# A recurrence feeding two gated MLPs on one core: the scratch word of the weight conversion moves to a PSUM bank, and two copies change their route

## The chip, the cores and the metric

One core of a Trainium2 chip runs the whole program. The metric is the device time of one execution in microseconds (us), lower is better. In the profile the engines are PE (TensorE), DVE (VectorE), ACT (ScalarE), POOL (GpSimd) and SP (SyncE, which here only issues DMAs; ACT issues DMAs too, and a letter q behind an engine's name stands for its sequencer).

## The reference

Batch 4, 8 heads, 768 time steps, head dimension 40. A linear recurrence gives one 320-wide row for each of 3072 tokens, and two MLPs follow on these rows.

```python
for t in range(S):
    y[:, :, t] = einsum('bhd,bhde->bhe', r_t, state)
    Sa = einsum('bhde,bhe->bhd', state, a_t)
    state = state * w_t - einsum('bhd,bhe->bhde', Sa, b_t) + einsum('bhd,bhe->bhde', v_t, k_t)
x = y.transpose(0, 2, 1, 3).reshape(3072, 320)
x = gate(x @ w_in) @ w_out                      # d_ff 2048; gate: 0, (h+1)^2/4 or h
out = (silu(x @ w_gate) * (x @ w_val)) @ w_out2  # d_ff 1536
```

The weights arrive as 8-byte numbers and are turned into float32 by bit operations, then into a high and a low float16 part.

## The kernel before

**Tiling.** Time is cut into 12 chunks of 64 steps. A chunk has four pieces of work, one for each batch entry, so there are 48 of them, numbered n = 4c + j. For each n, `p_tasks` prepares operands and the 64x64 products (tiles `ars`, `art`, `kbs`, `kbT`, `lkt`, `l21`), and `m_tasks` solves the triangular system of the chunk and carries the state on. For each chunk, `inv_tasks` inverts the 32x32 diagonal blocks of all 32 batch-head pairs in 62 short DVE instructions (lines 919 and 924), one pair behind the other. The two MLPs of a chunk (`in1`, `in2`, `outp`) follow when its rows are there: PE matmuls at lines 1181 and 1245, with ACT, DVE and POOL passes between them.

**Order.** All work is entered as tasks (engine, estimated cost, priority, buffers used) in a `Plan`. Its list scheduler runs when the program is built and fixes the order of every engine's instructions, from the costs written at each task and from pools of buffers; it repeats forward and backward passes and keeps the order with the earliest modelled end. A pool hands out a buffer in order of priority, and a task that finds none waits. DMAs go to SP's or ACT's queue, whichever the model finds free; on the chip each queue issues strictly in that order.

**The weights.** `wpiece` loads one of 58 pieces of raw words into a buffer of pool `wr` and works in three DVE instructions (`bits`, q = 0, 1, 2, lines 613, 617, 623): shift the upper word and mask it, put its top bits back, join the lower word's bits. By the code 20 pieces are 128x512, 28 are 128x320 and 10 are 128x256 (for those, line 623 runs twice on 64 partitions). The scratch word is the first part of the piece's buffer in pool `wu`, in SBUF, and the result of q = 2 goes to the same buffer. Then ACT (lines 643, 635) and POOL or DVE (lines 544, 546) split it into the two float16 parts.

**The solve.** Each `m_tasks` holds a PSUM bank of pool `px` (two banks; the first four solves may use the `ph` banks) from its first matmuls (line 1040) through two half solves: ACT line 1063, DVE and POOL copies of the half's right side, PE line 1050 with the inverse (`tt`), ACT line 1077 and DVE line 546 for the result, PE line 1056 between the halves. The inverse of a chunk goes from `ub` to DRAM (`tsd`, four copies, line 945) and back to `tt` (two copies for each pair of solves, lines 1011 and 1015). At its end a solve leaves the new state: `ss` by ACT and DVE, a transposed copy `s0t` (line 1154), and a stack `s0s` of three blocks of 40 partitions (high, low, high part) made from a POOL copy into `sr` (line 1158, high and low part) and three copies from SBUF to SBUF (line 1163). The solve n + 4 reads `s0s` at line 1133.

**Buffers around it.** `art`, `kbs`, `lkt` and `l21` have six buffers each, and two more (one for `lkt`) that serve n = 4 to 7 at the start and n >= 8 only once `pad` has run, which waits for the last weights. So until then the preparation of n needs the buffers of the solve n - 6.

Of the kernel before, what the change touches and what calls it, by code (L numbers as in the profile page):

```python
# [9 lines left out]
F16 = mybir.dt.float16  # L10
# [312 lines left out]
def tile_recurrence__then__gated_mlps(  # L323
# [64 lines left out]
    def pst(name, n):  # L388
        ts = [pp.tile([128, 512], F32, name=f"{name}{i}") for i in range(n)]
        K.pool(name, ts)  # L390
        return ts
# [28 lines left out]
    sbt("xs", [128, H, D], F16, 2)  # L420
    sbt("tt", [128, 2, 2, H, HC], F16, 1)
    gfs = sbt("gf", [128, H, C], F32, 1)
    K.pool("sr", [gfs[0][0:D].bitcast(F16).rearrange("p h t -> p (h t)")[:, 0:2 * HD].rearrange(
        "p (l h d) -> p l h d", l=2, h=H)])
    sbt("pf", [128, H, C], F32, 1)
    mx = sbt("mx", [128, 36 * NT], F16)
    K.pool("xt", [mx[:, 6 * NT * i:6 * NT * (i + 1)].rearrange("p (a t) -> p a t", a=6)
# [27 lines left out]
            "p (h x) -> p h x", h=H)], early)  # L455
    K.spare("gf", [mx[:, 7168:8192].bitcast(F32).rearrange("p (h t) -> p h t", h=H)], early)
    px = pst("px", 2)
    pst("pg", 2)
    ph = pst("ph", 2)
    po = [pp.tile([128, 512], F32, name=f"po{i}") for i in range(2)]  # L460
# [57 lines left out]
    def c_ps(n):  # L518
        return 0.14 + n * 0.9e-3

    def DMA(emit, dma, cost=0.78, **kw):
        T("DQ", cost, lambda q: emit(nc.scalar if q == "ACT" else nc.sync), dma=dma, **kw)
# [62 lines left out]
    def wpiece(names, key, src, n, m, dst_hi, dst_lo, scale, p, fit, r=()):  # L585
# [3 lines left out]
            "low": (0,), "high": (1,), "free": (2,), "late": (3, 4)}[f]]  # L589
        K.pools["wu"]["fit"][key] = [x for f in fit for x in {  # L590
            "low": (0, 4), "high": (1, 5), "free": (2,), "late": (3,)}[f] if m <= 320 or x < 4]
        raw, ux = [("wr", key)], [("wu", key)]
        shape = list(dst_hi.shape)

# [13 lines left out]
            e.dma_start(out=G("wr", key)[:, 0:2 * mw].bitcast(I32), in_=src)  # L608

        def bits(q):  # L610
            t = G("wu", key)[:, 0:mw].bitcast(I32)
            if q == 0:
                v_.tensor_scalar(  # L613
                    out=t, in0=x(1), scalar1=3, scalar2=0x3FFFFFFF,
                    op0=ALU.logical_shift_left, op1=ALU.bitwise_and)
            elif q == 1:
                v_.scalar_tensor_tensor(  # L617
                    out=t, in0=x(1), scalar=-(1 << 30), in1=t, op0=ALU.bitwise_and,
                    op1=ALU.bitwise_or)
            else:  # L620
                for i in range(2 if low else 1):
                    z = slice(64 * i, 64 * i + 64) if low else slice(0, 128)
                    v_.scalar_tensor_tensor(  # L623
                        out=u().bitcast(I32)[:, i * mw:i * mw + mw], in0=x(0)[z], scalar=29,
                        in1=t[z], op0=ALU.logical_shift_right, op1=ALU.bitwise_or)
# [10 lines left out]

        DMA(load, r=r, w=[(key, 0)], use=raw, p=p, dma=0.00365 * m * n / 128)
        for q in range(3):
            T("DVE", (0.08 + mw * 0.52e-3, 0.06 + mw * 1.04e-3, (0.21 if low else 0.06) + m * 1.04e-3)[q],
              lambda q=q: bits(q), r=[(key, q)],  # L640
              w=[(key, q + 1)], use=raw + ux, p=p)
        if pool:
            T("ACT", c_s(m), lambda: s_.activation(
                out=u(), in_=u(), func=AF.Copy, scale=scale0), r=[(key, 3)], w=[(key, 4)], use=ux, p=p)
# [243 lines left out]

    def inv_tasks(c, p):
        key = ("i", c)  # L890
        tsd[c] = dr.tile([2, 2, HC, BH, HC], F16, name=f"tsd{c}")
        ub, pm = [("ub", key)], [("pg", key)]

        def L():
# [8 lines left out]
        def T16():  # L903
            return G("ub", key)[:, 0:512].bitcast(F16).rearrange(
                "p (l m t) -> p l m t", l=2, t=HC)
# [34 lines left out]
        T("DVE", c_v(512), lambda: split(T16()[:, 1], M(), 2.0**8, T16()[:, 0]),  # L940
          r=[(key, "h")], w=[(key, "l")], use=ub + pm, p=p)

        def st(e, g, hf):
            l0 = 64 * g + 32 * hf
            e.dma_start(
                out=tsd[c].rearrange("f l (m g) b t -> f g b l m t", g=2)[hf, g],
                in_=T16()[l0:l0 + 32])

        for g in range(2):
            for hf in range(2):  # L950
                DMA(lambda e, g=g, hf=hf: st(e, g, hf), r=[(key, "l")], w=[("tsd", c)], use=ub,
                    p=p - 20, dma=0.73, cost=0.68)

    def x_tile(name, key):
        t = G(name, key)
# [24 lines left out]
    def m_tasks(n, p):  # L980
# [15 lines left out]
        if j % 2 == 0:  # L996
# [8 lines left out]
            if not last:  # L1005
# [4 lines left out]
            td = tsd[c][:, :, :, ps]  # L1010
            DMA(lambda e: e.dma_start(
                out=G("tt", mp)[0:64].rearrange("p f j h t -> p f (j h t)"),
                in_=td.rearrange("f l s b t -> (l s) f (b t)")),
                r=[("tsd", c)], w=[(mp, "tt")], use=TT, p=p - 3, dma=0.5)
            DMA(lambda e: e.dma_start(
                out=G("tt", mp)[64:96].rearrange("p f j h t -> p f (j h t)"),
                in_=td[:, 0].rearrange("f s b t -> s f (b t)")),
                r=[("tsd", c)], w=[(mp, "tt")], use=TT, p=p - 3, dma=0.25, cost=0.68)

        T("ACT", c_s(HD), lambda: s_.activation(  # L1020
# [116 lines left out]
        if not last:  # L1137
            y = lambda: hd(G(pg, (key, "y")))[q]
            if c:
# [15 lines left out]
                out=s0t[j], in_=flat(G("ss", key)[64:112])),  # L1155
                r=[("ss", n)], w=[("s0t", n)], use=SS, p=p, dma=0.57)
            SR = [("sr", key)]
            T("Pool", c_ps(2 * HD), lambda: p_.tensor_copy(
                out=G("sr", key),
                in_=G("ss", key)[q, :, 0:2 * D].rearrange("p h (l d) -> p l h d", l=2)),  # L1160
              r=[("ss", n)], w=[(key, "sr")], use=SS + SR, p=p + 8)
            for i in range(3):
                DMA(lambda e, i=i: e.dma_start(
                    out=s0s[j][D * i:D * i + D], in_=G("sr", key)[:, i % 2]),
                    r=[(key, "sr")], w=[("s0s", n)], use=SR, p=p + 8, dma=0.12, cost=0.45)
        xk = ("x", c, j // 2)
        xf = lambda: G("pf", (key, "x"))[vr].rearrange("p h t -> p (h t)")[:, 0:HD]
        XF = [("pf", (key, "x"))]
# [123 lines left out]
    for i in range(NP1):  # L1292
# [4 lines left out]
        for x in ps:  # L1297
            n = len(first)
            first.append(wpiece(
                *x, p=-WLEAD + WSTEP * n, fit=("low", "high", "free") if n < NW1 else ("low", "high")))  # L1300
    late, low, high = [], list(first), list(first)
    free = [("dec", c) for c in range(NCH)] + [("f", c) for c in range(NCH - 1)] + first[:NW1]
    for i, k in W2:
        if k < 2:
# [105 lines left out]
```

## Time and profile before

| | us |
|---|---|
| median of three runs | 1190.2 (1187.24 to 1194.36) |
| the profiled execution, its time | 1187.51 |
| the profiled execution, its span | 1185.5 |
| PE busy in the span | 914.2 (77%) |
| DVE busy | 808.5 (68%) |
| ACT busy | 738.7 (62%) |
| POOL busy | 707.6 (60%) |

The span is cut into stretches with different limits: the first 380 us, in which weights are converted; the middle, in which chunks follow one another at an even pace; and the end, in which only MLPs are left. Busy shares are to be read for each stretch alone. "The chain of work that ended last" follows the last instruction back through what released each step, so an engine's or line's share of it is the part of the span that it holds up.

### The profile page before, as it was taken

How to read it: one execution, taken by the hardware profiler on the slowest of the kernel's cores; microseconds unless marked ns; L12 is line 12 of the kernel's file. 1: busy time of each engine (PE TensorE's matmuls, PEld its weight loads, DVE VectorE, ACT ScalarE, POOL GpSimd, SP SyncE). 2: the span in 40 equal slices, each digit the busy share in tenths (PEclk: the TensorE clock that was granted, in tenths of full speed). 3: DMA queues.
4: the chain of work that ended last, by engine and by line, in shares of the span. 5: the costliest groups of instructions: out<-in, count | busy, mean ns of one | idle time of the engine just before them, and what ended most of it. 6: DMA issues, size and time to landing. Idle time of an engine off the chain costs nothing.

```text
span 1185.5 us, 29632 instructions
## 1 busy us (share of the span) xinstructions
PE 914.2 (77%) x11328; PEld 746.2 (63%) x11328; DVE 808.5 (68%) x1888; ACT 738.7 (62%) x1380; POOL 707.6 (60%) x952
## 2 busy tenths in 40 slices
PE   0321245645668698899998989999999899999998
PEld 0220233434457477677776777778778778788887
DVE  8779896998978677486684784867848668442111
ACT  0874575655676576775866857768668675553422
POOL 4698758544668567566675666676666644342321
PEclk9999999767989899999999999999999999999999
DMA  7954776738676757676567586774766743211000
GB/s 218 229 155 124 224 153 146 175 96 179 163 152 140 152 101 141 139 124 135 104 120 127 113 134 126 129 152 94 133 120 132 123 93 67 66 18 30 12 14 23
DMA packets 381522, 144.61 MB, mean 122 GB/s; under 512 B 345140, under 2 KB 358100, under 8 KB 381380
## 3 DMA queue, kind: packets, MB, share of 16 engines
q1 hardware_dynamic: 364416, 126.34, 51.3%
q10 hardware_dynamic: 16964, 16.39, 6.1%
q8 instruction: 88, 1.44, 0.5%
q14 instruction: 54, 0.44, 0.1%
HBM read 74.87 MB, written 18.14 MB: 78 GB/s over the span
## 4 chain that ended last, share of the span: by engine, by line
DVE 29%; PE 24%; DMA 15%; ACT 10%; POOL 9%; issue 7%; SPq 4%; ACTq 1%; POOLq 0%; DVEq 0%
PE ph L1181 12%; PE po L1245 9%; DVE pg L924 3%; DVE ub L919 3%; DMA ub<-lsd 3%; DVE vss L546 3%; DMA x2t<-mx 2%; DVE wo L623 2%; POOL ldp L550 2%; DVE wo L617 2%; DVE mx L1217 1%; DMA tsd<-ub 1%; POOL wv L550 1%; ACT ss L1146 1%; DVE wo L613 1%
## 5 line engine op out<-in xcount | busy, mean ns | idle before, releaser
L1245 PE MATMUL po<-wo,mx 128*128 128x320 f16 x2016 | 310.6, 302 | 15.8 <-POOL mx L544 8.4
L544 POOL TENSOR_TENSOR mx<-mx 128x512 f16<-128x512 f32 x168 | 196.6, 1172 | 188.8 <-ACT mx L1201 177.0
L1245 PEld LDWEIGHTS <-mx 128*128 128x128 f16 x2016 | 191.6, 98 | 88.2 <-POOL mx L544 11.2
L1181 PE MATMUL ph<-mx,w 128*128 128x256 f16 x1536 | 201.6, 285 | 54.7 <-DVE mx L1217 33.3
L1181 PEld LDWEIGHTS <-w 128*128 128x128 f16 x1536 | 150.7, 101 | 81.5 <-issue 53.5
L1201 ACT CAST mx<-mx 128x512 f16<-128x512 f32 x168 | 102.5, 615 | 81.3 <-DVE mx L1231 38.5
L1181 PE MATMUL ph<-x2t,wv 128*128 128x256 f16 x1152 | 140.2, 272 | 3.8 <-DVE mx L1231 3.1
L1181 PE MATMUL ph<-x2t,wg 128*128 128x256 f16 x1152 | 139.5, 272 | 2.7 <-DVE mx L1217 1.4
L1217 DVE SCALAR_TENSOR_TENSOR mx<-ph,mx 128x512 f32<-128x512 f32 x96 | 66.0, 688 | 91.2 <-ACT mx L1214 90.7
L1181 PEld LDWEIGHTS <-wv 128*128 128x128 f16 x1152 | 110.8, 98 | 17.9 <-issue 4.6
L1181 PEld LDWEIGHTS <-wg 128*128 128x128 f16 x1152 | 109.5, 98 | 17.1 <-issue 2.9
L919 DVE SCALAR_TENSOR_TENSOR ub<-ub,pg 128x126 f32<-128x126 f32 (+22 forms) x372 | 91.4, 246 | 15.3 <-DMA ub<-lsd 7.9
L924 DVE TENSOR_TENSOR pg<-pg,ub 128x126 f32<-128x126 f32 (+22 forms) x372 | 95.2, 256 | 7.1
L1231 DVE SCALAR_TENSOR_TENSOR mx<-ph,mx 128x512 f32<-128x512 f32 x72 | 49.3, 685 | 70.7 <-PE ph L1181 66.7
L550 POOL TENSOR_TENSOR ldp<-ldp 64x320 f32<-64x320 f32 (+1 forms) x90 | 79.8, 894 | 12.0 <-DMA ldp<-was 7.2
L1077 ACT ACTIVATE vss<-px 32x640 f16<-32x640 f32 x88 | 59.9, 693 | 28.0 <-PE px L1050 20.2
L1213 ACT ACTIVATE mx<-ph 128x512 f32<-128x512 f32 x96 | 57.1, 595 | 27.1 <-PE ph L1181 20.4
L1050 PEld LDWEIGHTS <-tt 96*32 96x32 f16 x768 | 26.2, 95 | 72.9 <-DMA tt<-tsd 36.9
L546 DVE SCALAR_TENSOR_TENSOR vss<-px,vss 32x320 f16<-32x320 f32 x88 | 43.4, 493 | 39.0 <-ACT vss L1077 36.4
L1227 ACT ACTIVATE mx<-ph 128x512 f32<-128x512 f32 x72 | 42.8, 595 | 35.0 <-PE ph L1181 33.5
L1068 POOL COPY xs<-xs 32x320 f16<-32x320 f16 x89 | 41.9, 472 | 37.0 <-ACT xs L1063 33.5
L1214 ACT ACTIVATE mx<-mx 128x512 f32<-128x512 f32 x96 | 60.5, 630 | 3.1
(238 smaller groups left out, 1784.7 us busy)
## 6 DMA issues: line engine op xcount, KB each, us to landing
ldp<-in_kb_dram SPq DMA_DIRECT2D x21, 320.0 KB
ub<-lsd SPq DMA_DIRECT2D x19, 256.0 KB
ldp<-in_ar_dram ACTq DMA_DIRECT2D x15, 320.0 KB
ldv<-in_v_dram SPq DMA_DIRECT2D x14, 320.0 KB
wo<-in_wo_dram SPq DMA_DIRECT2D x14, 320.0 KB
wo<-in_w1a_dram SPq DMA_DIRECT2D x8, 512.0 KB
ldp<-wks SPq DMA_DIRECT2D x23, 160.0 KB
sf<-was SPq DMA_DIRECT2D x23, 160.0 KB
```

The costliest lines, as they stand in the source:

```text
L544: e.tensor_tensor(out=out, in0=x, in1=hi, op=ALU.subtract)
L546: e.scalar_tensor_tensor(out=out, in0=x, scalar=scale, in1=hi, op0=ALU.mult, op1=ALU.subtract)
L550: e.tensor_tensor(out=out, in0=x, in1=y, op=ALU.mult)
L919: v_.scalar_tensor_tensor(out=t, in0=L()[:, j, j + 1:].unsqueeze(1).to_broadcast([128, nm, ni]), scalar=-(2.0**-10), in1=m[:, 0:nm, j:j + ...
L924: v_.tensor_tensor(out=m[:, 0:nm, j + 1:], in0=m[:, 0:nm, j + 1:], in1=t, op=ALU.add)
L1077: s_.activation(out=hi2(G("vss", key)[z]), in_=two(hd(G("px", key))[z]), func=AF.Copy, scale=2.0**-8)
L1181: t_.matmul(out=ps, lhsT=wts[:, wi, fs], rhs=xT[:, xi, :], start=(i == 0), stop=(i == len(plan) - 1))
L1201: T("ACT", c_s(512) - 0.04, lambda: s_.copy(out=G("g", key)[:, 0], in_=u2(key)), r=[(key, "u")], w=[(key, "gh")], use=U + GG, p=p)
L1213: s_.activation(out=u2(key), in_=ps2(key), func=AF.Relu, scale=2.0**-8, bias=1.0)
L1214: s_.activation(out=u2(key), in_=u2(key), func=AF.Square, scale=2.0**3)
L1217: T("DVE", c_v(512, True), lambda: v_.scalar_tensor_tensor(out=u2(key), in0=ps2(key), scalar=2.0**8, in1=u2(key), op0=ALU.max, op1=ALU.min ...
L1245: t_.matmul(out=ps, lhsT=g[:, x, f, 128 * tt:128 * tt + 128], rhs=wo[:, 2 * i + f, y, :], start=(i == 0 and f == 0 and m == 0), stop=(i == ...
```

## The change

Three things are changed. (1) The scratch word of the weights is a tile of a new pool `pw`, which is the second bank of `px`; `px` starts with one bank and gets the second back when the last weights are done. The `wu` buffer is taken only at q = 2. (2) `tsd` has another layout, and the inverse is written to it by two copies of 64 partitions in place of four of 32. (3) The POOL copy writes three blocks in place of two, one copy takes them to a DRAM tile `sdr`, and a second copy brings them back as the stack of 120 partitions. Some cost estimates of the planner are changed with them.

```diff
+    K.pools["px"]["free"] = px[0:1]
+    K.any("pw", px[1:2], (0,))
...
         def bits(q):
-            t = G("wu", key)[:, 0:mw].bitcast(I32)
+            t = G("pw", key)[:, 0:mw].bitcast(I32)
...
-            T("DVE", (0.08 + mw * 0.52e-3, 0.06 + mw * 1.04e-3, (0.21 if low else 0.06) + m * 1.04e-3)[q],
+            T("DVE", (0.06 + mw * 1.04e-3, 0.06 + mw * 1.04e-3, (0.21 if low else 0.06) + m * 1.04e-3)[q],
               lambda q=q: bits(q), r=[(key, q)],
-              w=[(key, q + 1)], use=raw + ux, p=p)
+              w=[(key, q + 1)], use=raw + [("pw", key)] + (ux if q == 2 else []), p=p)
...
-        tsd[c] = dr.tile([2, 2, HC, BH, HC], F16, name=f"tsd{c}")
+        tsd[c] = dr.tile([2, HC, 2, BH, HC], F16, name=f"tsd{c}")
...
         for g in range(2):
-            for hf in range(2):
-                DMA(lambda e, g=g, hf=hf: st(e, g, hf), r=[(key, "l")], w=[("tsd", c)], use=ub,
-                    p=p - 20, dma=0.73, cost=0.68)
+            DMA(lambda e, g=g: e.dma_start(
+                out=tsd[c].rearrange("l (m g) f b t -> g (f b) (l m) t", g=2)[g],
+                in_=T16()[64 * g:64 * g + 64].rearrange("p l m t -> p (l m) t")),
+                r=[(key, "l")], w=[("tsd", c)], use=ub, p=p - 20, dma=1.4, cost=0.75)
...
-            T("Pool", c_ps(2 * HD), lambda: p_.tensor_copy(
+            T("Pool", c_ps(3 * HD), lambda: p_.tensor_copy(
                 out=G("sr", key),
-                in_=G("ss", key)[q, :, 0:2 * D].rearrange("p h (l d) -> p l h d", l=2)),
+                in_=G("ss", key)[q, :, 0:3 * D].rearrange("p h (l d) -> p l h d", l=3)),
               r=[("ss", n)], w=[(key, "sr")], use=SS + SR, p=p + 8)
-            for i in range(3):
-                DMA(lambda e, i=i: e.dma_start(
-                    out=s0s[j][D * i:D * i + D], in_=G("sr", key)[:, i % 2]),
-                    r=[(key, "sr")], w=[("s0s", n)], use=SR, p=p + 8, dma=0.12, cost=0.45)
+            sdr = dr.tile([3, D, HD], F16, name=f"sdr{n}")
+            DMA(lambda e: e.dma_start(
+                out=sdr.rearrange("l p x -> p l x"), in_=G("sr", key).rearrange("p l h d -> p l (h d)")),
+                r=[(key, "sr")], w=[(key, "sd")], use=SR, p=p + 8, dma=0.36, cost=0.5)
+            DMA(lambda e: e.dma_start(
+                out=s0s[j][0:3 * D].rearrange("p h d -> p (h d)"), in_=sdr.rearrange("l p x -> (l p) x")),
+                r=[(key, "sd")], w=[("s0s", n)], p=p + 8, dma=0.36, cost=0.5)
...
     late, low, high = [], list(first), list(first)
+    K.grow("px", px[1:2], late)
```

## Rows read from the trace of the kernel before

**Rows 1.** Busy time by stretch: engine, us, instructions; then PEclk, DMA share, GB/s.
```profile
200.00:300.00 100.00, 54.55 (x668) 42.18 (x665) 91.17 (x185) 61.48 (x117) 55.53 (x63) 0.76 0.63 148
300.00:380.00 80.00, 57.91 (x712) 45.29 (x712) 71.26 (x126) 56.16 (x110) 58.60 (x69) 0.91 0.70 149
500.00:1000.00 500.00, 468.17 (x6129) 386.13 (x6128) 356.08 (x869) 350.48 (x672) 316.69 (x403) 1.00 0.63 120
1000.00:1186.00 186.00, 179.62 (x1814) 147.48 (x1811) 51.90 (x96) 78.20 (x145) 55.17 (x60) 1.00 0.15 30
```

**Rows 2.** The chain that ended last, 100 to 380 us, shares by line.
```profile
by line: issue 8.9%; DVE wo L623 7.8%; DVE wo L617 6.5%; DVE wo L613 4.9%; POOL wv L550 4.2%; PE ph L1181 3.6%; DVE pg L924 3.6%; DVE ub L919 3.5%; DVE lsp L617 3.2%; DVE vss L546 3.1%; DVE lsp L623 2.8%; DMA kbT<-kbs 2.5%; DVE lsp L613 2.1
```

**Rows 3.** DVE busy in lines 613, 617, 623, one after the other.
```profile
sum 400.00, DVE 31.57; mean DVE 15.78
...
sum 400.00, DVE 44.58; mean DVE 22.29
...
sum 400.00, DVE 51.53; mean DVE 25.77
```

**Rows 4.** The same lines: ns min/median/max, first and last start; single 512s from the timeline.
```profile
L613 DVE TENSOR_SCALAR wo<-wo x32: 276/420/1182, 27.3 to 321.7; 128x320 int32<-128x320 int32 x13, 128x512 int32<-128x512 int32 x12, 128x256 int32<-128x256 int32 x7
L613 DVE TENSOR_SCALAR lsp<-lsp x11: 313/427/932, 276.8 to 374.3; 128x320 int32<-128x320 int32 x8, 128x512 int32<-128x512 int32 x3
...
302.37 1.52 DVE L617 SCALAR_TENSOR_TENSOR lsp<-wo,lsp 128x512 int32<-128x512 int32 x1
323.34 0.67 DVE L623 SCALAR_TENSOR_TENSOR lsp<-lsp 128x512 int32<-128x512 int32 x1
329.55 0.43 DVE L613 TENSOR_SCALAR lsp<-lsp 128x512 int32<-128x512 int32 x1
```

**Rows 5.** DVE groups by line and form: busy us, mean ns, idle before.
```profile
L1217 DVE SCALAR_TENSOR_TENSOR mx<-ph,mx 128x512 f32<-128x512 f32 x96 | 66.0, 688 | 91.2 <-ACT mx L1214 90.7
L546 DVE SCALAR_TENSOR_TENSOR vss<-px,vss 32x320 f16<-32x320 f32 x88 | 43.4, 493 | 39.0 <-ACT vss L1077 36.4
L546 DVE SCALAR_TENSOR_TENSOR vss<-ldv,vh 128x320 f16<-128x320 f32 x48 | 41.9, 873 | 3.7 <-ACT vh L1020 2.3 <-DMA vsT<-vss 0.9
```

**Rows 6.** Timeline (start us, us): solves 6, 8 and 9, what reads 9, inverse 3.
```profile
208.83 0.36 PE L1040 MATMUL px<-vh,lkt 128*128 128x40 f16 x8
225.94 0.50 DVE L546 SCALAR_TENSOR_TENSOR vss<-px,vss 32x320 f16<-32x320 f32 x1
...
295.31 0.57 PE L1050 MATMUL px<-xs,tt 96*32 96x40 f16 x16
309.07 0.50 DVE L546 SCALAR_TENSOR_TENSOR vss<-px,vss 32x320 f16<-32x320 f32 x1
314.74 0.50 DVE L546 SCALAR_TENSOR_TENSOR vss<-px,vss 32x320 f16<-32x320 f32 x1
336.48 0.36 PE L1133 MATMUL pg<-s0s,art 120*128 120x40 f16 x8
401.88 0.69 DVE L546 SCALAR_TENSOR_TENSOR ub<-pg,ub 128x512 f16<-128x512 f32 x1
```

**Rows 7.** DMA issues on the queues: ns min/median/max; the last, who waited longest.
```profile
L1163 SPq DMA_DIRECT2D s0s<-gf x67: 706/761/1253, 152.0 to 995.6; - x67
L1163 ACTq DMA_DIRECT2D s0s<-gf x65: 719/737/1331, 150.5 to 1005.2; - x65
L1006 SPq DMA_DIRECT2D ldp<-fdr x21: 289/461/467, 24.6 to 974.5; - x21
...
SPq L908 <- DMA lsd<-gf: 7.0, 2, 3.9
```

**Rows 8.** The chain that ended last, around 790 us, and POOL's copy for the stack.
```profile
786.35 0.78 ACTq L1163
790.88 2.10 SPq L945
...
L1158 POOL COPY gf<-ss x41: 712/713/977, 184.1 to 1002.9; 40x640 f16<-40x640 f16 x41
```

More of the change, by code (lines that the diff above doesn't have):

```diff
@@ L422, in tile_recurrence__then__gated_mlps @@
     gfs = sbt("gf", [128, H, C], F32, 1)
-    K.pool("sr", [gfs[0][0:D].bitcast(F16).rearrange("p h t -> p (h t)")[:, 0:2 * HD].rearrange(
-        "p (l h d) -> p l h d", l=2, h=H)])
+    K.pool("sr", [gfs[0][0:D].bitcast(F16).rearrange("p h t -> p (h t)")[:, 0:3 * HD].rearrange(
+        "p (l h d) -> p l h d", l=3, h=H)])
     sbt("pf", [128, H, C], F32, 1)
@@ L591, in wpiece @@
             "low": (0, 4), "high": (1, 5), "free": (2,), "late": (3,)}[f] if m <= 320 or x < 4]
+        K.pools["pw"]["fit"][key] = (0,)
         raw, ux = [("wr", key)], [("wu", key)]
@@ L941, in inv_tasks @@
           r=[(key, "h")], w=[(key, "l")], use=ub + pm, p=p)
[L943 to L947, printed above, removed]
         for g in range(2):
-            for hf in range(2):
-                DMA(lambda e, g=g, hf=hf: st(e, g, hf), r=[(key, "l")], w=[("tsd", c)], use=ub,
-                    p=p - 20, dma=0.73, cost=0.68)
+            DMA(lambda e, g=g: e.dma_start(
+                out=tsd[c].rearrange("l (m g) f b t -> g (f b) (l m) t", g=2)[g],
+                in_=T16()[64 * g:64 * g + 64].rearrange("p l m t -> p (l m) t")),
+                r=[(key, "l")], w=[("tsd", c)], use=ub, p=p - 20, dma=1.4, cost=0.75)
     def x_tile(name, key):
@@ L1012, in m_tasks @@
                 out=G("tt", mp)[0:64].rearrange("p f j h t -> p f (j h t)"),
-                in_=td.rearrange("f l s b t -> (l s) f (b t)")),
+                in_=td.rearrange("l s f b t -> (l s) f (b t)")),
                 r=[("tsd", c)], w=[(mp, "tt")], use=TT, p=p - 3, dma=0.5)
@@ L1016, in m_tasks @@
                 out=G("tt", mp)[64:96].rearrange("p f j h t -> p f (j h t)"),
-                in_=td[:, 0].rearrange("f s b t -> s f (b t)")),
+                in_=td[0].rearrange("s f b t -> s f (b t)")),
                 r=[("tsd", c)], w=[(mp, "tt")], use=TT, p=p - 3, dma=0.25, cost=0.68)
```

## The prediction

> **What bounds the kernel now.** I read the busy times by stretch first [rows 1]. From 1000 us on PE is busy for 179.6 of 186 us, and from 500 to 1000 us for 468 of 500: there the MLPs' matmuls set the pace, and at most 32 us of gaps are left in those 500 us. From 200 to 300 us it is another kernel: PE 55, DVE 91 of 100 us. So a saving in the first 380 us counts if DVE, or what waits behind DVE, gets shorter, and after that nearly only what fills a gap on PE.
>
> The second view is the chain that ended last, cut to 100 to 380 us [rows 2]. The three lines that turn weight words into floats (L613, L617, L623) hold 4.9 + 2.1, 6.5 + 3.2 and 7.8 + 2.8 per cent of it, 27.3% of 280 us or 76 us. The inverse's own steps (L919, L924) have 7.1%. The reason is the order: between two short steps of an inverse DVE runs one weight instruction, and the inverse waits for it.
>
> The third view is the duration of these instructions [rows 3, 4]. All of them lie before 380 us and take 31.57 + 44.58 + 51.53 = 127.68 us. One form has very unequal durations: a 128x512 of L617 takes 1.52 us at 302 us, while one of L623, the same kind of instruction, takes 0.67; L613 on 128x320 goes from 0.313 to 0.93 us or more. Instructions with one operand in PSUM don't spread: L1217 (128x512) has a mean of 688 ns over 96, L546 on the solve's bank (32x320) 493 over 88, and L546 with both inputs in SBUF (128x320) has 873 [rows 5]. What is paid there beyond the plain duration is a stop by POOL, which works on SBUF at the same time.
>
> **The bit word in PSUM.** With the scratch word in PSUM, q = 1 and q = 2 have one input in SBUF and one in PSUM, as L1217 has, so I price a 128x512 at 688 and a 128x320 at 493 ns [rows 5]; a straight line through both gives 428 for 256. With 20, 28 and 10 pieces, L617 is 13.76 + 13.80 + 4.28 = 31.84 us, and L623 is 13.76 + 13.80 + 20 x 0.428 = 36.12. For q = 0 the trace shows no instruction with one SBUF source that writes PSUM. Its bounds are its own undisturbed durations of 427, 313 and 276 ns [rows 4], 20.06 us in all, and the PSUM prices above, 31.84 us. I take the upper one, as its rows are those that touch PSUM. Then the three lines cost 99.80 us, 27.9 less than 127.68. With the lower price it is 39.7 less. If the stops by POOL stayed, it would be 127.68 + 31.84 - 20.06, 11.8 more than now.
>
> On that one term a page has an opinion. L613 takes 427 ns for the 512 elements for which L623 needs 670 [rows 4]. The Trainium skill's page "VectorE: DVE Perf Modes", section "Mode 2×_2P — use both read ports for one tensor", says that a one-source instruction gets its double rate only while source and destination are both in SBUF. By it the saving is 27.9 us, without it 39.7; no row here shows such an instruction with a PSUM destination.
>
> Of the 127.68 us, 76 are on the chain, so a cut of 27.9 / 127.68 = 22% is worth 16.7 us there. POOL, which is stopped in its turn, gains a little too; I put that at nothing, as POOL is only 56 to 73% busy there [rows 1].
>
> **The lent bank.** Until the last weights are done (about 380 us) all solves but the first four share one bank, and a solve's first matmuls wait until the one before has read its last result. Queued behind them on PE are matmuls of the MLPs and of later preparations, in the order that the planner gives. The place to look at is chunk 2 [rows 6]: its inverse is first used at 295.3 us, and solves 8 and 9, both with their first matmuls long done, run side by side, last results at 309.07 + 0.50 = 309.6 and 314.74 + 0.50 = 315.2. With one bank, 9 starts at 309.6. A solve that runs alone takes from 208.83 to 226.44, 17.6 us, so 9 ends at 327.2, 12 us late. Who waits: solve 9's outputs are read at 336.5, which frees the buffers for the preparation of n = 15, and on that hangs the inverse of chunk 3, split at 401.9. The pair 4 and 5 of chunk 1 runs into the same, but its delay is mostly taken up before 6 and 7 are needed. Against these 12 us: solve 8 has the engines to itself, and DVE puts weights forward in the gaps, which would have come later. Bounds 0 and 12; I take 7, a bit over the middle, as DVE has only 9% of slack in the stretch before and 11% in this [rows 1].
>
> **The two copies of the inverse.** Two issues fewer in each of 12 chunks. The longest issue on the chain there is 2.10 us [rows 8], against 461 ns for a small copy [rows 7]: the queue is held up by the number of 64-byte runs, and this is the same for two copies as for four. I count the pieces of L945 on the chain from 470 us on at 12.6 us in five chunks, take 2 off, and keep 0 and 6 as bounds.
>
> **The stack through DRAM.** 132 issues of 761 ns (SP) and 737 ns (ACT) [rows 7], 99 us of queue time, become 88. A copy between SBUF and DRAM of about this size has 461 ns as a median [rows 7], which makes 41 us; at the old price it is 66. On the chain L1163 has 28 pieces, of which the longest stands there with 0.78 us [rows 8], 10.6 us in all; a third to half goes, 4 us. POOL's copy grows by half at most, 0.36 us x 44 = 16 us [rows 8]; it is covered by the time that the state has until the next chunk's solve reads it, and without that cover it would cost 0.36 us each. The new wait is the copy back, which waits on its queue for the copy out. Behind it on SP stand the transposes (L776, L976, L1154), on ACT the solve's activations, and PE waits for these. The nearest rows for a copy that waits for another through DRAM are L908's: 7.0 us in two waits, up to 3.9 [rows 7], out of 24 such copies, so 0.3 us on average, 13 us for 44 copies, if each hits the chain; I take 1.
>
> **The sum.** -16.7 + 7 - 2 - 4 + 1 = -14.7 us. A part of it falls into gaps that PE has anyway: PE is 94% busy from 500 us [rows 1], so an earlier start is kept but savings of the queues are not all; I keep three quarters, -11. The profiled execution took 1187.5, so 1176.5; the median of the runs shown is 2.7 above it, so **1179 us**, 0.9% less than 1190.2. The planner orders everything anew, with priorities fitted to the old costs; from the profile this has no sign, and I allow 6 us either way.
>
> **The rivals.**
> *The bank sets the pace (slower).* Solve 9 is 12 us late with all of it passed on, and since DVE is full, its later steps queue behind weights as they do now; the pair of chunk 1 adds a quarter of the same, 3 us. Then chunk 3's inverse is late by 15 us, and what DVE saves is spent on weights off the chain, with 5 us of the 16.7 kept: 1190.2 + 15 - 5 = 1200. It decides as soon as the delay of a pair's second solve is more than what the weights gave back before it. For it: from 295 to 402 us the order is solve, preparation, inverse, with no slack between them in the buffers. Against it: a pair meets only where both solves stand ready before the inverse, in two chunks of the three that fall into the lent time. The Trainium skill's page "Perfetto Trace Analysis", section "Matmul Optimizations", asks for all eight PSUM banks to be used so that independent work overlaps; this change goes against it, and the side by side run of solves 8 and 9 is what it means here.
> *Nothing to measure.* Relief and bank cancel, 1188 to 1192.
> *More.* q = 0 keeps its speed and the bank costs nothing: 39.7 x 76 / 127.7 = 24 us plus 5 of the queues, 1162.
> *The copy back holds its queue.* If 44 copies cost up to 1.3 us each on ACT or SP and half of it hits the chain, 29 us come on top of the forecast: 1208.
>
> **How the numbers follow.** Forecast (1170 to 1184) 0.42, more (1158 to 1170) 0.10, nothing 0.22, bank 0.21, queue 0.05. 0.5% is 6 us, about what can be told from no change here. Faster is 0.42 + 0.10 = 0.52, same 0.22, slower 0.26. The range 1163 to 1204 leaves out about 0.04 below and 0.08 above; the forecast's own is 1170 to 1184.
>
> **What would show it.** L617 and L623 without spread, at 0.69 us for 512; the three lines at about 100 us; L613 near its PSUM or its old price. In the lent time no two solves between L1040 and the last L546 at once; inverse 3 split before 402 us if I am right, after it if the bank decides. Fewer ACT issues, and L1163's successor at about 0.5 us. I am wrong if inverse 3 comes earlier and the end does not, which would mean that PE or POOL alone set the pace from there on, or if a wait of the copy back stands among the longest of SP's or ACT's queue.

## The result, and the profile after

The changed kernel takes 1134.8 us (median of four, 1131.7 to 1145.29) against 1188.7 for the kernel before: a ratio of 0.9564, interval 0.950 to 0.963. The direction was forecast and the size was not: 0.9% forecast, 4.4% measured, and the time lies below the range. The profiled execution of after is the slowest of its four (1145.29, span 1142.7), so the spans differ by 42.8 us and the medians by 53.9.

Busy times of after by stretch, as in [rows 1] (us and instructions of PE, weight loads, DVE, ACT, POOL; then PEclk, DMA share, GB/s):

```profile
200.00:300.00 100.00, 57.43 (x719) 43.41 (x717) 87.20 (x200) 66.56 (x128) 55.57 (x67) 0.74 0.68 168
300.00:380.00 80.00, 62.12 (x731) 48.40 (x729) 63.24 (x151) 55.80 (x107) 57.76 (x77) 0.94 0.80 156
500.00:1000.00 500.00, 477.75 (x6195) 395.09 (x6194) 344.36 (x853) 352.82 (x670) 317.82 (x395) 0.99 0.65 122
1000.00:1143.00 143.00, 139.10 (x1332) 115.08 (x1329) 29.99 (x48) 53.66 (x98) 39.07 (x42) 1.00 0.09 20
```

From 300 to 380 us DVE has fallen from 71 to 63 of 80 us. From 500 to 1000 us PE has 9.6 us more work in the same time.

The three weight lines of after (ns min/median/max, first and last start), as in [rows 4]:

```profile
L616 DVE TENSOR_SCALAR px<-wo x38: 419/495/696, 27.4 to 310.7; 128x320 int32<-128x320 int32 x17, 128x512 int32<-128x512 int32 x15, 128x256 int32<-128x256 int32 x6
...
L620 DVE SCALAR_TENSOR_TENSOR px<-wo,px x38: 422/495/697, 28.1 to 312.2; 128x320 int32<-128x320 int32 x17, 128x512 int32<-128x512 int32 x15, 128x256 int32<-128x256 int32 x6
L620 DVE SCALAR_TENSOR_TENSOR px<-lsp,px x16: 428/496/696, 265.8 to 343.9; 128x320 int32<-128x320 int32 x9, 128x512 int32<-128x512 int32 x4, 128x256 int32<-128x256 int32 x3
...
L626 DVE SCALAR_TENSOR_TENSOR wo<-wo,px x39: 407/486/689, 28.8 to 313.4; 128x320 int32<-128x320 int32 x16, 128x512 int32<-128x512 int32 x13, 64x256 int32<-64x256 int32 x10
```

The spread is gone: 697 ns is the longest. Before, [rows 4] have a shift of 1182 ns and a single L617 of 1.52 us, and the longest in that trace are a shift of 1.38 and an L623 of 1.90 us. Added up over the span the lines take 31.68 + 31.79 + 35.65 = 99.1 us; 99.80 was forecast.

The timeline of after (start us, us) around solves 8 and 9, as in [rows 6]: first matmuls of solve 8, split of inverse 2, last result of 8, first matmuls of 9, last result of 9, first matmuls of 10, split of inverse 3.

```profile
247.12 0.36 PE L1038 MATMUL px<-vh,lkt 128*128 128x40 f16 x8
...
253.21 0.69 DVE L548 SCALAR_TENSOR_TENSOR ub<-pg,ub 128x512 f16<-128x512 f32 x1
...
285.82 0.50 DVE L548 SCALAR_TENSOR_TENSOR vss<-px,vss 32x320 f16<-32x320 f32 x1
...
286.37 0.36 PE L1038 MATMUL px<-vh,lkt 128*128 128x40 f16 x8 [0.42 <-DVE vss L548]
...
310.18 0.50 DVE L548 SCALAR_TENSOR_TENSOR vss<-px,vss 32x320 f16<-32x320 f32 x1
...
310.73 0.37 PE L1038 MATMUL px<-vh,lkt 128*128 128x40 f16 x8 [1.05 <-DVE vss L548]
...
374.20 0.69 DVE L548 SCALAR_TENSOR_TENSOR ub<-pg,ub 128x512 f16<-128x512 f32 x1 [0.67 <-ACT ub L940]
```

Each solve now begins 0.05 us after the last result of the one before it: the bank is handed on, and no two stand side by side. Yet inverse 3 is split at 374.2 us, 27.7 us earlier than at 401.88 [rows 6].

The copies of after: the inverse's (L947), POOL's copy for the stack (L1156), the stack out to DRAM (L1161) and back (L1164), as in [rows 7, 8]:

```profile
L947 SPq DMA_DIRECT2D tsd<-ub x23: 603/640/3545, 108.1 to 972.6; - x23
...
L1156 POOL COPY gf<-ss x41: 979/981/1134, 170.6 to 963.7; 40x960 f16<-40x960 f16 x41
...
L1161 SPq DMA_DIRECT2D sdr<-gf x24: 284/410/1561, 139.1 to 885.6; - x24
L1161 ACTq DMA_DIRECT2D sdr<-gf x20: 280/292/330, 155.6 to 964.7; - x20
...
L1164 SPq DMA_DIRECT2D s0s<-sdr x28: 327/384/1313, 159.2 to 946.0; - x28
...
L1164 ACTq DMA_DIRECT2D s0s<-sdr x16: 333/342/608, 141.2 to 967.0; - x16
```

The stack's issues take 0.29 to 0.41 us (medians) where each of three took 0.74 to 0.76: by the medians some 32 us of queue time in place of 99, added up one by one 37 in place of 100. The copy back waits for the copy out (SP's longest waits, us in total, times, longest):

```profile
SPq L1164 <- DMA sdr<-gf: 18.9, 14, 2.3
```

That is 18.9 us on a queue that waits anyway, never more than 2.3 at once. It is the tenth of SP's waits by total, so one of the signs that the prediction named for being wrong is there. The chain that ended last is no help in after: it breaks off at 870 us, so the comparison goes by stretches and by the start of one instruction, the split of each chunk's inverse (DVE, `ub<-pg,ub` 128x512).

### The profile page after: what moved, and what is told of

Its sections match the earlier page's. It is cut to its first block, busy times and chain, and to the rows that moved or that the text cites. A ratio compares the mean times of both kernels' runs of the same rounds, so it can differ in the third digit from the quotient of the medians.

```text
span 1142.7 us, 29552 instructions
## 1 busy us (share of the span) xinstructions
PE 911.7 (80%) x11328; PEld 745.7 (65%) x11328; DVE 770.7 (67%) x1888; ACT 741.3 (65%) x1380; POOL 697.3 (61%) x952
## 5 line engine op out<-in xcount | busy, mean ns | idle before, releaser
L1182 PE MATMUL ph<-mx,w 128*128 128x256 f16 x1536 | 204.0, 287 | 51.0 <-DMA mx<-x 35.5
L552 POOL TENSOR_TENSOR ldp<-ldp 64x320 f32<-64x320 f32 (+1 forms) x90 | 76.8, 862 | 13.7 <-DMA ldp<-was 10.7
L1228 ACT ACTIVATE mx<-ph 128x512 f32<-128x512 f32 x72 | 43.0, 598 | 38.3 <-PE ph L1182 36.5
L1156 POOL COPY gf<-ss 40x960 f16<-40x960 f16 x41 | 40.4, 985 | 34.0 <-issue 13.8
```

The lines of the kernel that those rows point to most:

```text
L552: e.tensor_tensor(out=out, in0=x, in1=y, op=ALU.mult)
L1182: t_.matmul(out=ps, lhsT=wts[:, wi, fs], rhs=xT[:, xi, :], start=(i == 0), stop=(i == len(plan) - 1))
```

## The parts one by one

Six kernels with one, two or all of the three parts, each against runs of the kernel before on the same chip. The two right columns are starts of the split of inverse 3 and inverse 11 in the profiled execution.

| kernel | parts | us (median) | less than before | inverse 3 | inverse 11 |
|---|---|---|---|---|---|
| before | none | 1188.7 | | 401.9 | 1011.9 |
| after | word, inverse, stack | 1134.8 | 53.9 | 374.2 | 971.2 |
| only_word | word | 1164.6 | 24.4 | 373.4 | 997.1 |
| only_inv | inverse | 1190.8 | -1.8 | 406.6 | 1012.7 |
| only_stack | stack | 1161.6 | 27.4 | 396.7 | 986.3 |
| no_word | inverse, stack | 1169.1 | 19.9 | 400.9 | 994.5 |
| word_stack | word, stack | 1134.2 | 55.2 | 370.9 | 963.2 |

Ratios with intervals: only_word 0.9803 (0.976 to 0.985), only_inv 1.0025 (1.000 to 1.005), only_stack 0.9785 (0.976 to 0.981), no_word 0.9819 (0.979 to 0.985), word_stack 0.9523 (0.947 to 0.957).

**only_word**: the hunks of part (1) alone, the core of which is

```diff
-            t = G("wu", key)[:, 0:mw].bitcast(I32)
+            t = G("pw", key)[:, 0:mw].bitcast(I32)
```

> The kernel before with the first part of the change alone: scratch word in the lent PSUM bank, the copies as before. Contention theory (the stops by POOL are what is saved, on DVE and on POOL): the three weight lines at 99 us in place of 127.7, inverse 3 split 20 to 28 us before the 401.9 of before, time 1148 to 1165 us, ratio 0.966 to 0.98. Copies theory (freed queues give most): 1175 or more, ratio over 0.988. Bank theory (one bank costs, and the copies hide it): 1190 or more.

It brings inverse 3 forward by 28 us, as in after, and then gives half of that back: 15 us are left at inverse 11. The profiled execution is the slowest of its four, though (1172.4, 8 us above their median), so a part of this belongs to the one execution.

**no_word**: parts (2) and (3), with the word in SBUF as before.

> The kernel before with the two copies alone: inverse in two copies, stack through DRAM, scratch word in SBUF as before. Contention theory: the weight lines stay at 125 to 130 us, time 1168 to 1185 us, ratio 0.983 to 0.997, the gain after 400 us. Copies theory: 1130 to 1150 us, ratio about 0.96.

Nothing is gained up to inverse 3 (1 us), and 17 us by inverse 11: the copies quicken the pace where the prediction had PE set it. **only_inv** and **only_stack** take this apart.

> The kernel before with the second part alone: the inverse goes to DRAM in two copies of 64 partitions. Both copies alone gave 1169.1 against 1189.0, all of it after the split of inverse 3 at 401 us. Theory I (the inverse's way to the solves is what PE waits for between chunks): this part carries it, 1165 to 1176, and from the split of inverse 3 to that of inverse 11 it takes 592 to 600 us in place of 610. Theory S (what counts is the 67 us of issue time that the stack's copies no longer take on ACT and SP): 1183 to 1191 and 606 to 612 us. Theory H (each gives a part): 1176 to 1183.

> The kernel before with the third part alone: the stack goes through DRAM in one copy out and one back. Theory S: 1167 to 1177, with 592 to 600 us from the split of inverse 3 to that of inverse 11. Theory I: 1183 to 1191 and 606 to 612 us. Theory H: 1176 to 1183. If the copy back held its queue, as one of my rivals had it, it would be 1190 or more.

All of it is the stack, and the inverse's two copies are worth nothing: theory S, though with more than it named (1161.6 where 1167 to 1177 was expected). From inverse 3 to 11 only_stack takes 589.6 us, before 610.0, only_inv 606.1. **word_stack**, the changed kernel with the inverse's four copies back:

```diff
-        tsd[c] = dr.tile([2, HC, 2, BH, HC], F16, name=f"tsd{c}")
+        tsd[c] = dr.tile([2, 2, HC, BH, HC], F16, name=f"tsd{c}")
...
+            for hf in range(2):
+                DMA(lambda e, g=g, hf=hf: st(e, g, hf), r=[(key, "l")], w=[("tsd", c)], use=ub,
+                    p=p - 20, dma=0.73, cost=0.68)
```

> The changed kernel without its second part (the inverse goes to DRAM in four copies as before). Alone that part gave +2 us (1190.8 against 1189.1). If it gives nothing here either: 1130 to 1141. If it is needed once the other two have brought the solves forward (its queue is then fuller): 1142 to 1150.

It is level with after, so part (2) gives nothing beside the others either. The single parts add up: 24.4 + 27.4 - 1.8 = 50.0 of 53.9.

## How far the order alone moves the time

Every edit makes the planner order all instructions anew, so two edits change the order and no instruction. **cost_only** is the kernel before with the new price of the shift, **after_oldcost** the changed kernel with the old one:

```diff
-            T("DVE", (0.08 + mw * 0.52e-3, 0.06 + mw * 1.04e-3, (0.21 if low else 0.06) + m * 1.04e-3)[q],
+            T("DVE", (0.06 + mw * 1.04e-3, 0.06 + mw * 1.04e-3, (0.21 if low else 0.06) + m * 1.04e-3)[q],
```

> The kernel before, with only the planner's cost of the first bit instruction changed to the new value; what is computed and where stays as it is. It shows how far another order alone moves the time. Contention theory: within 1% of before, 1178 to 1200 us. Order theory: 1140 to 1165 us.

> The changed kernel with the planner's old cost of the shift instruction (0.35 in place of 0.59 us for 512), so another order of the same instructions. If the gain comes from the parts and not from one lucky order, 1129 to 1143; if the order of the changed kernel is a lucky one, 1150 or more. The same edit made to the kernel before gave 1185.1 against 1189.0.

cost_only 1185.1 (ratio 0.9969, 0.995 to 0.999), after_oldcost 1142.7 (0.9615, 0.958 to 0.965): 3.9 us down and, against after's 53.9, 7.5 up. A third edit of this kind (ws_acttime, below, in which 8 of ACT's 129 issues also go to SP) moves the time by 24.8. So a single difference below some 10 us is not read as the work of a part here, and one of 20 only with a second run that bears it out.

## Is it DVE's time?

**word_wu** is the changed kernel, bank lent and both copies changed, but with the word in the `wu` buffer in SBUF again:

```diff
-            t = G("pw", key)[:, 0:mw].bitcast(I32)
+            t = G("wu", key)[:, 0:mw].bitcast(I32)
...
-              w=[(key, q + 1)], use=raw + [("pw", key)] + (ux if q == 2 else []), p=p)
+              w=[(key, q + 1)], use=raw + [("pw", key)] + ux, p=p)
```

> The changed kernel, but the scratch word lies in the wu buffer in SBUF again (taken from q = 0 on); the bank stays lent, and the planner has the costs and pools of the changed kernel but for that buffer. Contention theory: the weight lines spread again, 127 us or more by their SBUF durations, and most of the gain goes, 1160 to 1190 us, ratio 0.975 to 1.0. Order theory (the planner's other order is what gains): 1130 to 1145 us, ratio 0.955 to 0.965.

1173.7 us (0.9868, 0.985 to 0.989), inverse 3 at 406.6: the place of the word is worth 39 us in the changed kernel. With the word in SBUF the spread is back, here in the second line of the three (ns min/median/max):

```profile
L620 DVE SCALAR_TENSOR_TENSOR wo<-wo x32: 426/618/1536, 28.4 to 328.7; 128x320 int32<-128x320 int32 x14, 128x512 int32<-128x512 int32 x13, 128x256 int32<-128x256 int32 x5
...
L620 DVE SCALAR_TENSOR_TENSOR wo<-lsp,wo x7: 493/959/2964, 290.1 to 338.7; 128x512 int32<-128x512 int32 x4, 128x320 int32<-128x320 int32 x3
```

Against no_word, which has both banks for the solves, word_wu is 4.6 us slower: that is the lent bank and another order together.

**twice_q0** is the changed kernel with the shift issued twice for each piece, in the same order and with nothing more in SBUF-to-SBUF form:

```diff
             if q == 0:
-                v_.tensor_scalar(
+                for _ in range(2):
+                    v_.tensor_scalar(
```

> The changed kernel with the shift instruction of each weight piece issued twice, in the same order of instructions: 31.7 us more on DVE before 380 us (58 pieces, the price measured in the changed kernel), all of it on instructions with one SBUF source and a PSUM destination, so POOL isn't stopped more. Theory D (until the weights are done DVE's time counts one for one): the split of inverse 3 moves from 374 us to 400 to 408, and the end by 20 to 32 us, 1155 to 1167. Theory C (as in my prediction, only the share on the chain of waits counts, 76 of 127.7): the split at 390 to 396 and the end at 1147 to 1155. Theory P (the gain was POOL's, which is stopped less, and DVE has room): the split before 384 and the end at 1132 to 1144.

The doubled line, DVE busy in the first 400 us (us, instructions):

```profile
0.00:400.00 400.00, 63.67 (x116) 0.90 0.70 167
```

63.67 in place of 31.68, 32.0 us more. The split of inverse 3 goes from 374.2 to 402.7, by 28.5, and the time to 1163.8 (0.9799, 0.977 to 0.983), 28.7 us less gain than after's: theory D. A microsecond on DVE before the weights are done costs 0.9 us at inverse 3; taking 28.6 away gave 27.7, 0.97. The chain's share (76 of 127.7, 0.6) is ruled out, and so is POOL's relief as the main cause, as POOL isn't stopped more by these instructions: the mean of its 14 TENSOR_TENSORs `wo<-wo,wo` of 128x320 before 400 us is 790 ns in twice_q0 and in after, against 843 before. That is the little that POOL did gain; its 124 of 128x80 gained 7 us in all.

The 0.97 is a net figure, and its closeness to one is in part luck. At inverse 2 after is 25.7 us ahead with 15.7 us less in the three lines (60.3 against 76.0); from there to inverse 3 the lines take 12.8 us less and only 2.0 are won, as solve 9 now waits for the bank. The 0.9 of twice_q0, with one bank on both sides, is the cleaner price.

## What the stack's copies cost

**Issue time.** **stack_load** is only_stack with the three SBUF to SBUF copies beside it, into a tile `scr` that nobody reads:

```diff
+            for i in range(3):
+                DMA(lambda e, i=i: e.dma_start(
+                    out=G("scr", (key, "d"))[D * i:D * i + D], in_=G("sr", key)[:, i % 2]),
+                    r=[(key, "sr")], use=SR + [("scr", (key, "d"))], p=p + 8, dma=0.12, cost=0.45)
```

> The kernel before with the stack through DRAM (1161.6 against 1189.1), and beside it the three SBUF to SBUF copies of each solve as they were (same shape, same priority, same cost to the planner), now into an unused tile that nobody reads. Theory Q (what the stack's new way saves is the issue time of those copies on ACT and SP, 99 us, in which their queues run nothing else): the time comes back, 1180 to 1192. Theory L (the new way brings the stack itself earlier or makes the order better, and issue time is hidden): 1158 to 1168. Between them, 1168 to 1180, both.

1192.4 (1.0026, 0.999 to 1.006): the gain is gone, with the new route in place. What it saved was the old copies, not the way to `s0s`: theory Q, at the upper edge of its range.

**The planner's price.** The planner counts 0.45 us for a copy that takes 0.74 to 0.76. **before_truecost** and **stack_load_true** change that number alone, in the kernel before and in stack_load:

```diff
-                    r=[(key, "sr")], w=[("s0s", n)], use=SR, p=p + 8, dma=0.12, cost=0.45)
+                    r=[(key, "sr")], w=[("s0s", n)], use=SR, p=p + 8, dma=0.12, cost=0.75)
```

> The kernel before with one number changed: the planner counts 0.75 us for each of the stack's three copies, what they take on the chip (737 to 761 ns), in place of 0.45. The instructions are the same, in another order. Theory Q: the issue time is paid in any order, 1182 to 1192. Theory O (the loss was the planner's, which counted 0.3 us too little 132 times and so placed them where they hurt): 1165 to 1180.

> The kernel with the stack through DRAM and the idle copies on either queue (1192.4), and the planner counts their right price, 0.75 us in place of 0.45. With the right price the same copies all on SP gave 1170.8, all on ACT 1201.6. If the wrong price is a good part of what they cost: 1165 to 1180. If it is the time on ACT alone (33 of the 99 us there, so a third of the way): 1178 to 1185. If neither, 1187 to 1197.

1177.9 (0.9907, 0.987 to 0.994) and 1178.7 (0.9952, 0.992 to 0.998): 11.6 us below before, and 10.8 less loss than stack_load. Twice the same size, so a part of the loss, though not most of it, was an order planned for too short an issue. 1178.7 lies in the range of the price and in that of the time on ACT (1178 to 1185), so by the time alone stack_load_true doesn't part them; but it has 57 of the 132 idle copies on ACT, stack_load 44, so it is not faster by less time on ACT.

**Which queue.** **load_act** and **load_sp** put the idle copies on one queue each, at the right price; **before_sp** puts the stack's own three copies on SP:

```diff
-                DMA(lambda e, i=i: e.dma_start(
+                T("ACT", 0.75, lambda i=i: nc.scalar.dma_start(
                     out=G("scr", (key, "d"))[D * i:D * i + D], in_=G("sr", key)[:, i % 2]),
-                    r=[(key, "sr")], use=SR + [("scr", (key, "d"))], p=p + 8, dma=0.12, cost=0.45)
+                    r=[(key, "sr")], use=SR + [("scr", (key, "d"))], p=p + 8, dma=0.12)
```

> The kernel before with the stack through DRAM, and beside it the three idle SBUF to SBUF copies of each solve, all on ACT's queue, at 0.75 us to the planner: 132 x 0.75 = 99 us more on ACT. On either queue as the planner liked (88 on SP, 44 on ACT) they cost 31 us, 1192.4 against 1161.6. Theory A (issue time costs where ACT's activations stand behind it): 1185 to 1220, more than load_sp. Theory S (it costs on SP, where the other transfers stand behind it): 1158 to 1172.

> The same three idle copies, all on SP's queue: 99 us more on SP, ACT untouched. Theory A: 1158 to 1172. Theory S: 1185 to 1220, more than load_act.

> The kernel before with the stack's three copies all on SP's queue, at 0.75 us to the planner: nothing of the stack is issued by ACT (65 x 0.74 = 48 us less on ACT, as much more on SP). The planner's right price alone gave 1177.9. Theory A: 1160 to 1174. Theory S: 1182 to 1200.

load_act 1201.6 (1.0101, 1.006 to 1.015), load_sp 1170.8 (0.9862, 0.983 to 0.989), before_sp 1167.5 (0.9834, 0.980 to 0.987). Against before of their own comparison they stand at +13.7, -17.1 and -20.4 us, and only_stack at -27.4: 132 idle copies cost 41 us on ACT and 10 on SP, the latter no more than an order makes. Theory A. The line of the idle copies in load_act and who waited for it (us, times):

```profile
L1164 ACTq DMA_DIRECT2D scr<-gf x132: 725/734/1742, 151.2 to 1028.1; - x132
...
who waited for it (us, times):
  ACT mx L1209: 16.8, 5
  ACT wt L1120: 9.1, 3
  ACT mx L1235: 6.7, 2
```

and in load_sp:

```profile
L1164 SPq DMA_DIRECT2D scr<-gf x132: 706/740/1837, 152.1 to 995.6; - x132
...
who waited for it (us, times):
  ACT wt L1120: 0.9, 1
  ACT mx L1221: 0.9, 1
```

The same instructions, as long; on ACT its activations stand behind them, on SP nearly nobody does. One spot of load_act's timeline (start us, us, in brackets the idle time before and what ended it):

```profile
717.75 2.31 ACTq L1164 DMA_DIRECT2D scr<-gf  x3
...
720.11 0.57 ACTq L1168 DMA_DIRECT2D sdr<-gf  x1
...
720.72 0.60 ACT L1235 ACTIVATE mx<-ph 128x512 f32<-128x512 f32 x1 [3.34 <-DMA scr<-gf]
...
721.35 0.69 DVE L1239 SCALAR_TENSOR_TENSOR mx<-ph,mx 128x512 f32<-128x512 f32 x1 [4.72 <-ACT mx L1235]
```

Three issues of 0.77 us and a fourth, with 0.37 us of waiting for POOL's copy ahead of them, hold ACT for 3.34 us, and DVE, which waits for ACT's result, for 4.72. The kernel before shows the same, smaller:

```profile
552.32 0.75 ACTq L1163 DMA_DIRECT2D s0s<-gf  x1
...
553.11 0.62 ACT L1201 CAST mx<-mx 128x512 f16<-128x512 f32 x1 [0.81 <-DVE ub L546]
553.14 0.73 ACTq L1163 DMA_DIRECT2D s0s<-gf  x1
...
553.87 1.16 POOL L544 TENSOR_TENSOR mx<-mx 128x512 f16<-128x512 f32 x1 [0.72 <-ACT mx L1201]
553.97 0.60 ACT L1227 ACTIVATE mx<-ph 128x512 f32<-128x512 f32 x1 [0.24 <-ACT mx L1201]
554.00 0.72 ACTq L1163 DMA_DIRECT2D s0s<-gf  x1
...
554.60 0.69 DVE L1231 SCALAR_TENSOR_TENSOR mx<-ph,mx 128x512 f32<-128x512 f32 x1 [1.57 <-ACT mx L1227]
```

The activation at 553.11 starts 0.04 us after the issue of 552.32 is over (the profile names a DVE instruction that ended at about the same time), the one at 553.97 0.10 us after the next issue, and POOL and DVE behind them idle for 0.72 and 1.57 us. An issue isn't lost time from end to end: the one at 553.14 starts while the activation of 553.11 still runs, and only what is left of it afterwards delays the next one. This view was there to be read; the prediction looked only at pieces on the chain. Where it ends up is PE, busy time from 380 to 1000 us (first pair), in before, only_stack and load_act:

```profile
380.00:1000.00 620.00, 569.03 (x7384) 467.00 (x7382) 434.81 (x1067) 429.61 (x819) 393.64 (x503) 0.99 0.64 123
```

```profile
380.00:1000.00 620.00, 598.45 (x7772) 496.78 (x7768) 444.81 (x1092) 444.93 (x848) 414.22 (x517) 0.99 0.70 130
```

```profile
380.00:1000.00 620.00, 567.85 (x7275) 462.90 (x7272) 421.15 (x1030) 425.92 (x814) 399.03 (x497) 0.99 0.66 130
```

569, 598 and 568 of 620 us; load_sp lies between, at 584. The stack's route puts 29 us more of PE's work into the same stretch, which is the 27 us of gain, and the idle copies on ACT take it out again.

By steps, the stack's 27.4 us are 11.6 for the price, 8.8 more for leaving ACT (before_sp), and 7.0 more for the short issues (only_stack). Only the sum, which other pairs of kernels bear out (word_stack against only_word 31, no_word against only_inv 22), and the difference between the two queues, 31 us, are larger than the 24.8 that another order made. The difference between the queues is one pair of runs, and it rests on the waits above as much as on its size; the division is not shown.

## Tries at a faster version, and what stays open

**ws_acttime**: word_stack, and in the planner's model an issue on ACT holds ACT for its whole price:

```diff
-                            busy[eng] = now + 0.1 if eng == "ACT" else end
+                            busy[eng] = end
```

> The changed kernel without its second part (1134.2), and in the planner's model a DMA that ACT issues holds ACT for the issue's whole cost, no longer for 0.1 us. The instructions are the same, in another order and with fewer DMAs on ACT. If the model's 0.1 us is what costs: 1118 to 1130, faster than both kernels. If the order is as good as it was: 1130 to 1140. If SP gets too full by it: 1140 to 1155.

1157.5 (0.9745, 0.971 to 0.978), a miss: 24.8 us behind word_stack, each against its own before. It lies outside all three ranges. Its issues on ACT add up to 46 us (word_stack 55) and on SP to 558 (547), so SP's queue is 11 us fuller over the whole span; whether that or the order makes the 24.8 us isn't settled.

**ws_sp** and **after_sp**: word_stack and after with the stack's two copies on SP alone:

```diff
-            DMA(lambda e: e.dma_start(
+            T("SP", 0.5, lambda: nc.sync.dma_start(
                 out=sdr.rearrange("l p x -> p l x"), in_=G("sr", key).rearrange("p l h d -> p l (h d)")),
-                r=[(key, "sr")], w=[(key, "sd")], use=SR, p=p + 8, dma=0.36, cost=0.5)
+                r=[(key, "sr")], w=[(key, "sd")], use=SR, p=p + 8, dma=0.36)
```

> The changed kernel without its second part (1134.2), and the stack's two copies (out to DRAM and back) on SP's queue alone. In the changed kernel 36 of these 88 stand on ACT, 20 x 0.28 + 16 x 0.33 = 11 us. By the slope of the idle copies on ACT (99 us cost 40) this is worth 4 us: 1126 to 1133, faster than both kernels, if ACT's issue time still counts. If the wait of the copy back now holds SP, on which nearly all other transfers stand: 1138 to 1150. Else 1133 to 1138.

> The same edit made to the changed kernel itself (1134.8), with the inverse in two copies. Expected as for the other: 1126 to 1133 if the 11 us on ACT still count, 1138 to 1150 if the copy back holds SP. If the two differ by more than 5 us, what is seen is the order of the instructions and not the queue.

1157.7 (0.9747, 0.970 to 0.979) and 1152.1 (0.9689, 0.965 to 0.973), slower than after by 22.3 and 16.7 us, each against its own before, and slower than any range that was named for them. The wait of the copy back in ws_sp:

```profile
SPq L1169 <- DMA sdr<-gf: 16.9, 20, 1.6
```

16.9 us in 20 waits, no more than after's 18.9 in 14. So the held queue isn't shown by its waits, and the two kernels differ by 5.6, the sign named beforehand for an effect of the order. Whether SP or the order costs here stays open; the short issues were not seen to be cheaper on SP than on ACT, against what the idle copies would make one expect. No version beat after beyond the measurement; word_stack equals it with less changed. All six kernels with word and stack changed (twice_q0, with its doubled work, aside) lie between 1134 and 1158, below the best with one of them (1161.6).

## Why the prediction was off, step by step

**The weight lines: right.** 99.1 against 99.80 us, and the shift took the PSUM price that was chosen (31.68 against 31.84). It takes 695 ns for 512 elements with a PSUM destination, 427 with one in SBUF [rows 4]; the Trainium skill's "VectorE: DVE Perf Modes", section "Mode 2×_2P — use both read ports for one tensor", agrees: it gives the double rate to operands in SBUF alone. That the spread goes with one operand out of SBUF agrees with "SBUF — State Buffer", section "Who interferes with whom", of the Trainium skill: a DVE instruction with two SBUF inputs contends with GpSimd's reads, one with at most one, outside the modes that use both ports, does not. That it was POOL that stopped these lines is borne out by POOL's own instructions, which got shorter too (843 to 790 ns); no run stilled POOL to show it.

**What they are worth: the first step that failed.** Of the saving only the chain's share was counted, 16.7 us; measured are 27.7 us at inverse 3, with the bank's loss already in it. The chain names the instructions that stood last, not those that count. On an engine that is 89 to 91% busy (DVE before, 200 to 380 us [rows 1]) and runs in order, a shorter instruction off the chain lets the next one on it start earlier, so the saving counts nearly whole.

**The lent bank: the mechanism came, and 7 us can't be told from nothing.** Solve 9's last result is read at 310.2 instead of 314.7, 4.5 us earlier, although inverse 2 is split 25.7 us earlier (278.95 to 253.21), so 21 us were lost by then: 4.6 on the inverse's way to solve 8, and 16.6 in the two solves, which now run one behind the other (from the first use of the inverse, 295.31 before and 274.19 after, 36.5 in place of 19.9 us), where the prediction had 12. It was right that inverse 3 hangs on solve 9's buffers: in both kernels the transposition into the freed `art` starts 0.07 us after the matmul is over that reads solve 9 last, and the inverse's input and first step follow (start us, us; before, whose matmul at 336.48 stands in [rows 6], then after, with the first use of inverse 2 on top):

```profile
336.91 1.25 SPq L776 DMA_TRANSPOSE art<-ars  x1
...
352.60 0.90 SPq L868 DMA_DIRECT2D lsd<-gf  x2
...
367.01 0.18 DVE L919 SCALAR_TENSOR_TENSOR ub<-ub,pg 128x31 f32<-128x31 f32 x1
```

```profile
274.19 0.37 PE L1048 MATMUL px<-xs,tt 96*32 96x40 f16 x8
...
317.79 0.36 PE L1131 MATMUL pg<-s0s,art 120*128 120x40 f16 x8
...
318.22 2.20 SPq L779 DMA_TRANSPOSE art<-ars  x1
...
330.00 0.83 SPq L871 DMA_DIRECT2D lsd<-gf  x2
...
341.82 0.18 DVE L922 SCALAR_TENSOR_TENSOR ub<-ub,pg 128x31 f32<-128x31 f32 x1
```

The loss is made up behind solve 9. From its last result to that matmul it takes 7.6 us in place of 21.7. In the 21.7 DVE is busy for 21.1, and 13.1 of them are weight lines; in the 7.6 these take 2.1, because 51 of the 58 shifts are done when solve 9 ends and not 47. This is what the prediction set against the 12 us, weights put forward in the gaps. From the matmul to the split another 9 us are won (56.4 in place of 65.4). As a price for the bank there is word_wu against no_word: 4.6 us slower, inverse 3 5.7 later. That is below what an order makes, so the 7 is neither shown nor refuted, and the same holds for the Trainium skill's rule to use all eight banks ("Perfetto Trace Analysis", section "Matmul Optimizations").

**The inverse's copies: small, as said.** Forecast -2 with bounds of 0 and -6; the runs show 0 within what an order makes. The reason given, that the number of 64-byte runs sets the issue, isn't borne out for single issues: 0.57 us is the median with 32 partitions (L945), 0.64 with 64 (L947), and equal issues differ (0.3 to 2.1 and 0.6 to 3.5 us).

**The stack: the largest error.** The issue price was nearly right (41 us of queue time forecast, 32 measured by the medians), its worth was not: -4 forecast, -27 measured. The pieces of L1163 on the chain add up to 10.6 us, and I took a third to a half of them. But an issue on ACT can delay the activation behind it, as in the two spots above, and such a delay shows as idle time of ACT, POOL, DVE and at last PE, and not as a piece of L1163.

**Three quarters passed on: wrong.** The saving was said to fall in part into gaps that PE has anyway. Before had 51 us of such gaps from 380 to 1000 us; they were the room for the gain, not a loss of it. The window from 500 us on left 19 of them out of sight.

**The rivals.** The bank didn't set the pace. The copy back held its queue for 18.9 us in all and the end didn't show it: the time fell although the sign that the prediction named for this rival, a place among SP's longest waits, was there. POOL's longer copy (713 to 981 ns, 12 us in all) isn't seen to cost anything. "More" had 24 us for the word, near the 24.4 of only_word, but by luck: it wanted the shift to keep its speed, and the shift took the PSUM price. It had the stack wrong like all the others.

## What to carry to other kernels

On an engine that is nearly full and runs in order, price a saving by its busy time, and not by the share of it on the chain. A DMA issue on an engine that also computes holds up what stands behind it there: sum the issues up by queue, and look in the timeline at what starts when an issue ends. When a planner makes the order, its prices for issues have to be those of the trace, and a difference of some 10 us between two orders says nothing about the edit.

## What the runs showed of the hardware

For the stack's copies the larger one is not the dearer one to issue: 40 partitions from SBUF to SBUF, 25 KB, take 0.74 to 0.76 us on either queue; three times as much from the same partitions to DRAM 0.29 on ACT and 0.41 on SP; and back to 120 partitions 0.34 and 0.38. Whether the route or the shape of the copy sets this price was not varied. The Trainium skill's "DMA: Bandwidth & Descriptors", section "Issuing engines are not separate DMA queues", calls the sequencer's time to start a DMA usually small relative to the DMA itself. No run here times these transfers to set beside their issues; the issues alone, 132 of 0.73 to 0.74 us or some 97 us, cost 41 us on ACT, and on SP 10, which an order can make.
